# Retention and soft mixture of experts: tiles of 128 positions of one batch in place of 64 positions of two

## The chip, the cores and the metric

The kernel runs on one core of one Trainium2 chip. The metric is the device time of one execution, in microseconds (us). A core has TensorE (PE, matmuls), VectorE (DVE), ScalarE (ACT), GpSimd (POOL) and SyncE (SP, which issues DMAs here). All of them run their own instruction streams and wait for each other by semaphores.

## The reference

`q`, `k` and `v` have 8 batches, 8 heads, 576 positions and 64 features per head, in fp32. The first half is causal attention without softmax, with a decay per head; the second half mixes all 4608 positions into 32 slots, runs 8 experts on 4 slots each, and mixes back:

```
scores = q @ k^T / 8                      # per batch and head
ret    = scores * gamma[h]**(i - j), 0 where j > i
x      = (ret @ v), heads side by side    # 4608 x 512
logits = x @ phi                          # 4608 x 32
d      = softmax of logits over the 4608 positions
slots  = d^T @ x                          # 32 x 512
e_out  = relu(slots[e] @ w1[e]) @ w2[e]   # 8 experts, F = 1024
c      = softmax of logits over the 32 slots
out    = c @ e_out                        # 4608 x 512
```

## The kernel before

**Tiles.** There are 36 tiles of 128 rows. A tile is 64 positions of two batches: rows 0 to 63 belong to one batch, 64 to 127 to the other. The order (`tile_order`) alternates between two pairs of batches. Each tile has 768 KB: keys (`kn`), queries transposed by the host (`qT`), values (`vn`). Four buffers `qb` take them in turn.

**One tile in the loop** (`for i in range(NT)`, L291):
- `k_transpose(i + 1)` (L138): four 128x128 transposes on PE into a `pt` buffer (pool `ps_t`, two buffers), and an ACT copy to `kts`.
- `scale` (L130): POOL multiplies the values by a decay table in place (L133), and builds a second table `xts` (L135) for every other tile.
- `inter` (L145): state of all earlier chunks times queries, 16 small matmuls in two calls, on quadrants of PE (64 rows by 64 columns); it is left out in the first chunk of a batch.
- `scores` (L159): 16 matmuls on quadrants, and a DVE multiplication by the causal mask (L168) to `sts`.
- `values` (L172): 16 matmuls on quadrants with the masked scores, on top of `inter`'s result; DVE multiplies by `xts` on the way out (L183) into a ring of eight tiles.
- `state` (L188): 16 matmuls on quadrants, keys times values, added up in PSUM; ACT copies the state to `sbs` (L203).

In fp32 each matmul call is two PE matmul instructions with a weight load each, and a transpose is one.

**One group of four tiles.** The soft mixture follows four tiles behind. In tile r of the next group:
- r = 0: `logits` (L220, four column strips), then the running maximum and `expo` on DVE and ACT (L238, with `alpha` in L241 and the running sum in L242)
- r = 1: `e_transpose` (L245)
- r = 2: `comb_1` (a transpose of the logits, then DVE and ACT up to the exponential) and at the tile's end `comb_2` (four DVE operations, L276 to L280)
- r = 3: `comb_3` first (the transpose L284 of the result `cn`, and an ACT copy), and at the tile's end `slot_sums` (L254, four column strips)

One `x_transpose` (L209, ACT copy L213) runs in each tile.

**What sets the order.** The schedule is manual: each engine runs its instructions in the order in which the program lists them. SP issues the load of tile i + 4 at the end of tile i, once `state` has read the buffer, and weight units (512 KB each) at a pace of 28 in 32 tiles. 39 of the 64 units are loaded before the expert stage; each unit used there makes room for another.

**Behind the loop** come the last group (logits, transposes, slot sums, the final softmax), the first expert layer (L419), the second (L440), and 18 `final` steps (L451), each with four calls on PE, an ACT copy, a DVE copy and an output DMA.

Of the kernel before, what the change touches and what calls it, by code (L numbers as in the profile page):

```python
# [20 lines left out]
NCH = S // 64  # L21
# [3 lines left out]
NW = 35  # L25
NR = 8
PACE = 30
# [3 lines left out]
def tile_order():  # L31
    return [(p0 + j, c) for p0 in (0, 2) for c in range(NCH) for j in range(2)]


@with_exitstack
def retention_softmoe(ctx, tc, qkv, wts, phi, mtab, vtab, gtab, ctab, msel, out):
# [10 lines left out]
    ps_t = ctx.enter_context(tc.tile_pool(name="ps_t", bufs=2, space=PS))  # L47
# [4 lines left out]
    qb = [const(f"qb{i}", 1536) for i in range(NQ)]  # L52
# [3 lines left out]
    kts = [const(f"kt{i}", 512) for i in range(2)]  # L56
    sts = [const(f"st{i}", 512) for i in range(2)]
    sbs = [const(f"sb{i}", 512) for i in range(2)]
    xts = [const(f"xt{i}", NP, 64) for i in range(2)]
    mt = const("mt", 64)  # L60
    vt = const("vt", NCH, H)
    gt = const("gt", NP, 64)
# [7 lines left out]
    ens = const("ens", P)  # L70
    nrun = [const(f"nrun{i}", 1) for i in range(2)]
    lrun = const("lrun", 1)

    nw = [0]

    def load_w(t):
        if nw[0] < 64:
            nc.sync.dma_start(out=t, in_=wts[nw[0]])
            unit_tile.append(t)
            nw[0] += 1  # L80
            return True
# [13 lines left out]
    load_t(2)  # L95
    load_t(3)
    load_w(ws[1])
# [6 lines left out]
    for _ in range(8):  # L104
        nc.tensor.matmul(pw[:, 0:P], lhsT=wz, rhs=wz, start=True, stop=True)

    def kn(t):
        return qb[t % NQ][:, 0:512]

    def qT(t):  # L110
        return qb[t % NQ][:, 512:1024].rearrange("p (a z i) -> p a z i", a=NP, z=2)

    def vn(t):
        return qb[t % NQ][:, 1024:1536].rearrange("p (h d) -> p h d", h=H)

    R = [slice(0, D), slice(D, P)]
    kT, sT, SX, xT = {}, {}, {}, {}
    sb = {}

    def S_of(t):  # L120
        return SX[t][:, :, 0:256].rearrange("p b (a i) -> p b a i", a=NP)

    def X_of(t):
        return SX[t][:, :, 256:512].rearrange("p b (s i) -> p b s i", s=NP)

    def alloc(t):
        if t not in SX:
            SX[t] = ps_x.tile([P, 2, 512], F32, name="sx")

    def scale(t):  # L130
        c = order[t][1]
        v = vn(t)
        nc.gpsimd.tensor_tensor(out=v, in0=v, in1=vt[:, c, :].unsqueeze(2).broadcast_to([P, H, D]), op=ALU.mult)  # L133
        if t % 2 == 0:
            nc.gpsimd.tensor_tensor(out=xts[t // 2 % 2], in0=gt, in1=cf[:, c, :].unsqueeze(2).broadcast_to([P, NP, 64]),  # L135
                                    op=ALU.mult)

    def k_transpose(t):  # L138
        pt = ps_t.tile([P, 512], F32, name="pt")
        for a in range(NP):  # L140
            nc.tensor.transpose(pt[:, a * P:(a + 1) * P], kn(t)[:, a * P:(a + 1) * P], ident)  # L141
        nc.scalar.copy(out=kts[t % 2], in_=pt)  # L142
        kT[t] = kts[t % 2].rearrange("p (a z s) -> p a z s", a=NP, z=2)

    def inter(t, swap):  # L145
        p, c = order[t]
        if c == 0:
            return
        alloc(t)
        x = X_of(t)  # L150
        sv = sb[p % 2].rearrange("p (z a d) -> p z a d", z=2, a=NP)
        for a0 in (0, 2):
            for j in range(2):
                z = j ^ swap
                for a in (a0, a0 + 1):
                    nc.tensor.matmul(x[R[a % 2], z, 2 * j + a // 2, :], lhsT=sv[R[j], z, a, :], rhs=qT(t)[R[j], a, z, :],  # L156
                                     start=(swap == 1 and a0 == 0), stop=True, skip_group_check=True)

    def scores(t):  # L159
        alloc(t)  # L160
        sp = S_of(t)
        for a in range(NP):
            for j in range(2):
                for z in range(2):
                    nc.tensor.matmul(sp[R[z], 1 - j, a, :], lhsT=kT[t][R[j], a, z, :], rhs=qT(t)[R[j], a, z, :],  # L165
                                     start=(order[t][1] == 0 and a == 0), stop=True, skip_group_check=True)
        st = sts[t % 2].rearrange("p (b a i) -> p b a i", b=2, a=NP)
        nc.vector.tensor_tensor(out=st, in0=sp, in1=mt.unsqueeze(1).unsqueeze(1).broadcast_to([P, 2, NP, 64]),  # L168
                                op=ALU.mult)
        sT[t] = st  # L170

    def values(t):  # L172
        c = order[t][1]
        x = X_of(t)
        v = vn(t)
        for j in range(2):
            for a0 in (0, 2):
                for z in range(2):
                    for a in (a0, a0 + 1):
                        nc.tensor.matmul(x[R[a % 2], z, 2 * j + a // 2, :], lhsT=v[R[z], 2 * a + j, :],  # L180
                                         rhs=sT[t][R[z], 1 - j, a, :], start=False, stop=True, skip_group_check=True)
        xT[t] = ring[t % NR]
        nc.vector.tensor_tensor(out=xT[t].rearrange("p (s z i) -> p z s i", s=NP, z=2), in0=x,  # L183
                                in1=xts[t // 2 % 2].unsqueeze(1).broadcast_to([P, 2, NP, 64]), op=ALU.mult)

    pst = {}

    def state(t):  # L188
        p, c = order[t]
        if c == NCH - 1:  # L190
            return
        if c == 0 and p % 2 == 0:
            pst[0] = ps_st.tile([P, 2, 2, NP, D], F32, name="pst")
        s = pst[0][:, :, p % 2]
        k = kn(t).rearrange("p (h d) -> p h d", h=H)
        v = vn(t)
        for a in range(NP):
            for z in range(2):
                for j in range(2):
                    nc.tensor.matmul(s[R[j], z, a, :], lhsT=k[R[z], 2 * a + j, :], rhs=v[R[z], 2 * a + j, :],  # L200
                                     start=(c == 0 and p % 2 == 0 and a == 0), stop=True, skip_group_check=True)
        sb[p % 2] = sbs[p % 2]
        nc.scalar.copy(out=sbs[p % 2].rearrange("p (z n) -> p z n", z=2), in_=s.rearrange("p z a d -> p z (a d)"))  # L203
# [83 lines left out]
    cn = const("cn", P)  # L287
    k_transpose(0)
    scale(0)
    scores(0)  # L290
    for i in range(NT):  # L291
        g, r = divmod(i - 4, 4)
        if g >= 0:
            if r == 0:
                logits(g)
            elif r == 1:
                e_transpose(g)
            elif r == 2:
                comb_1(g)
            else:  # L300
                comb_3(g)
# [3 lines left out]
        if g >= 0:  # L305
            x_transpose(i - 4)
            if r == 0:
                expo(g)
        inter(i, 0)
        values(i)  # L310
        if i + 1 < NT:
            inter(i + 1, 1)
        state(i)
        if i + 1 < NT:
            scores(i + 1)
        if g >= 0:
            if r == 2:
                comb_2(g)
            if r == 3:
                slot_sums(g)  # L320
# [222 lines left out]
```

## Time and profile before

| | |
|---|---|
| runs shown | 285.41 us median of 3, 283.62 to 285.42 |
| the profiled execution | 285.16 us |
| its span, first to last instruction | 283.4 us |
| PE busy | 216.8 us, 77% of the span |
| DVE, ACT, POOL busy | 93.1, 87.2, 51.5 us |
| mean granted PE clock | 0.869 of full speed |
| moved by DMA | 72.47 MB, 256 GB/s on average |

A line of the profile names the kernel's line, the engine, the operation, and the tiles written and read. PE is the matmul and PEld its weight load, which overlap. A busy PE is not PE at its peak, since matmuls are pipelined and their ends are modelled. "Issue" is time in which an engine waited for nothing that the profile shows. The clock has two levels, 1.2 and 2.4 GHz; a granted clock between them is a mean over time.

### The profile page before, as it was taken

To read this page: it belongs to the slowest core of one execution; us is meant where nothing else is said; L and a number is where in the kernel's file an instruction comes from. 1 tells how busy PE (TensorE), PEld (TensorE's weight loads), DVE (VectorE), ACT (ScalarE), POOL (GpSimd) and SP (SyncE) were. 2 spreads that over 40 slices of the span, in tenths; PEclk is the share of its full clock that TensorE was granted. 3 is DMA by queue.
4 is the path that set the end of the run, shared out by engine and by line. 5 is a ranking of instruction groups with operands and counts; after the bars stand their busy time and mean duration, and the time that the engine had idled before them with its cause. 6 is when DMAs were issued, how large, how long until landed. Compare 5 with 4: busy or idle time off the path is not lost.

```text
span 283.4 us, 12138 instructions
## 1 busy us (share of the span) xinstructions
PE 216.8 (77%) x5594; PEld 157.7 (56%) x5594; DVE 93.1 (33%) x193; ACT 87.2 (31%) x192; POOL 51.5 (18%) x63
## 2 busy tenths in 40 slices
PE   6776977787857976856697588784694989898793
PEld 6665766665647765745676466664562224443451
DVE  0232233335423354522253343341455001033331
ACT  2131533343422243422253334242141000134321
POOL 1533223121321233221112132130021000000000
PEclk9597797999985697997799999899797799999655
DMA  6977685467774478555566749789220499999985
GB/s 212 415 286 242 209 335 193 182 221 273 275 279 158 161 229 324 189 187 187 187 205 234 248 180 289 269 301 388 97 79 1 140 415 407 408 409 412 422 358 225
DMA packets 18196, 72.47 MB, mean 256 GB/s; under 512 B 2401, under 2 KB 2785, under 8 KB 18145
## 3 DMA queue, kind: packets, MB, share of 16 engines
q1 hardware_dynamic: 17568, 71.47, 68.9%
q8 instruction: 44, 0.72, 1.0%
q10 hardware_dynamic: 576, 0.22, 0.3%
q14 instruction: 8, 0.06, 0.1%
HBM read 62.25 MB, written 9.44 MB: 253 GB/s over the span
## 4 chain that ended last, share of the span: by engine, by line
PE 70%; issue 12%; DVE 11%; ACT 3%; DMA 2%; SPq 0%; ACTq 0%; DVEq 0%
PE sx L156 8%; PE sx L180 7%; PE sx L458 7%; PE sx L165 7%; PE pt L209 7%; PE pst L200 7%; PE pst L419 6%; PE pt L141 5%; PE pt L440 5%; DVE st L168 5%; PE pt L254 4%; PE pt L224 3%; DMA qb<-in_qkv 2%; PE pt L284 1%; DVE csm L277 1%
## 5 line engine op out<-in xcount | busy, mean ns | idle before, releaser
L133 POOL TENSOR_TENSOR qb<-qb,vt 128x512 f32<-128x512 f32 x36 | 37.5, 1042 | 134.4 <-DMA qb<-in_qkv 110.9
L183 DVE TENSOR_TENSOR rg<-sx,xt 128x512 f32<-128x512 f32 x36 | 24.8, 690 | 65.8 <-PE sx L180 65.8
L168 DVE TENSOR_TENSOR st<-sx,mt 128x512 f32<-128x512 f32 x36 | 24.9, 691 | 48.9 <-PE sx L165 48.9
L165 PE MATMUL sx<-qb,kt 64*64 64x64 f32 x1152 | 29.0, 237 | 11.6 <-issue 10.9
L203 ACT COPY sb<-pst 128x512 f32<-128x512 f32 x32 | 18.7, 585 | 53.8 <-PE pst L200 53.8
L200 PE MATMUL pst<-qb 64*64 64x64 f32 x1024 | 26.0, 236 | 12.1 <-issue 12.1
L156 PE MATMUL sx<-qb,sb 64*64 64x64 f32 x1024 | 31.9, 239 | 3.8 <-issue 2.8
L165 PEld LDWEIGHTS sx<-qb,kt 64*64 64x64 f32 x1152 | 25.2, 152 | 12.4 <-issue 11.5
L156 PEld LDWEIGHTS sx<-qb,sb 64*64 64x64 f32 x1024 | 24.0, 147 | 10.9 <-issue 9.1
L141 PE MATMUL pt<-ident,qb 128*128 128x128 f32 x144 | 26.6, 313 | 4.5 <-DMA qb<-in_qkv 2.6
L200 PEld LDWEIGHTS pst<-qb 64*64 64x64 f32 x1024 | 22.2, 151 | 13.1 <-issue 13.1
L180 PE MATMUL sx<-st,qb 64*64 64x64 f32 x1152 | 27.2, 238 | 0.2 <-issue 0.2
L209 PE MATMUL pt<-ident,rg 128*128 128x128 f32 x132 | 23.9, 310 | 4.6 <-DVE cn L270 4.4
L142 ACT COPY kt<-pt 128x512 f32<-128x512 f32 x36 | 20.9, 581 | 18.2 <-PE pt L141 18.2
L180 PEld LDWEIGHTS sx<-st,qb 64*64 64x64 f32 x1152 | 23.8, 154 | 1.5 <-issue 0.8
L458 PE MATMUL sx<-kt,lt 32*128 32x256 f32 x144 | 22.0, 548 | 2.5 <-ACT kt L449 0.9
L141 PEld LDWEIGHTS pt<-ident,qb 128*128 128x128 f32 x144 | 18.9, 159 | 7.5 <-issue 5.2
L209 PEld LDWEIGHTS pt<-ident,rg 128*128 128x128 f32 x132 | 17.0, 159 | 8.5 <-PE pt L141 6.7
L213 ACT COPY rg<-pt 128x512 f32<-128x512 f32 x33 | 19.4, 587 | 2.7 <-PE pt L209 2.5
L458 PEld LDWEIGHTS sx<-kt,lt 32*128 32x128 f32 x144 | 10.9, 233 | 13.4 <-ACT ws L460 6.1
L284 PE MATMUL pt<-ident,cn 128*128 128x128 f32 x9 | 3.3, 365 | 18.6 <-DVE cn L280 18.6
L461 DVE COPY ws<-sx 128x512 f32<-128x512 f32 x14 | 9.7, 692 | 23.1 <-PE sx L458 21.2
(79 smaller groups left out, 188.3 us busy)
## 6 DMA issues: line engine op xcount, KB each, us to landing
ws<-in_wts SPq DMA_DIRECT2D x60, 512.0 KB, 7.0
qb<-in_qkv SPq DMA_DIRECT2D x35, 768.0 KB, 4.7
out<-ws SPq DMA_DIRECT2D x14, 512.0 KB, 9.4
qb<-in_wts SPq DMA_DIRECT2D x4, 512.0 KB, 4.2
out<-qb SPq DMA_DIRECT2D x4, 512.0 KB, 5.2
qb<-in_qkv SPq DMA_DIRECT2D x3, 256.0 KB, 3.3
gt<-in_gtab ACTq DMA_DIRECT2D x1, 128.0 KB, 7.1
ms<-in_msel SPq DMA_DIRECT2D x1, 96.0 KB, 6.3
```

The source lines that it names most:

```text
L133: nc.gpsimd.tensor_tensor(out=v, in0=v, in1=vt[:, c, :].unsqueeze(2).broadcast_to([P, H, D]), op=ALU.mult)
L141: nc.tensor.transpose(pt[:, a * P:(a + 1) * P], kn(t)[:, a * P:(a + 1) * P], ident)
L142: nc.scalar.copy(out=kts[t % 2], in_=pt)
L156: nc.tensor.matmul(x[R[a % 2], z, 2 * j + a // 2, :], lhsT=sv[R[j], z, a, :], rhs=qT(t)[R[j], a, z, :], start=(swap == 1 and a0 == 0), sto ...
L165: nc.tensor.matmul(sp[R[z], 1 - j, a, :], lhsT=kT[t][R[j], a, z, :], rhs=qT(t)[R[j], a, z, :], start=(order[t][1] == 0 and a == 0), stop=T ...
L168: nc.vector.tensor_tensor(out=st, in0=sp, in1=mt.unsqueeze(1).unsqueeze(1).broadcast_to([P, 2, NP, 64]), op=ALU.mult)
L180: nc.tensor.matmul(x[R[a % 2], z, 2 * j + a // 2, :], lhsT=v[R[z], 2 * a + j, :], rhs=sT[t][R[z], 1 - j, a, :], start=False, stop=True, sk ...
L183: nc.vector.tensor_tensor(out=xT[t].rearrange("p (s z i) -> p z s i", s=NP, z=2), in0=x, in1=xts[t // 2 % 2].unsqueeze(1).broadcast_to([P, ...
L200: nc.tensor.matmul(s[R[j], z, a, :], lhsT=k[R[z], 2 * a + j, :], rhs=v[R[z], 2 * a + j, :], start=(c == 0 and p % 2 == 0 and a == 0), stop ...
L209: nc.tensor.transpose(pt[:, a * P:(a + 1) * P], xT[t][:, a * P:(a + 1) * P], ident)
L213: nc.scalar.copy(out=xT[t], in_=pt)
L458: nc.tensor.matmul(po[i // 2][:, i % 2, 0:W], lhsT=lt[r, g, :], rhs=so[r, lo:hi], start=True, stop=True, tile_position=(i * NS, 0), skip_g ...
```

## The change

A tile is now 128 positions of one batch. Chunks 0 to 3 of a batch have such tiles, alternately for the two batches of a pair (z = 0, 1); chunk 4 has the last 64 positions of both batches (z = 2). There are still 36 tiles.

- Scores: the 128x128 matrix of a head lies in quadrants. Where the keys are the tile's later half, only the later half of the queries is computed (64 columns instead of 128). The host swaps the key halves of every second pair of heads, so that these blocks take turns between the column halves of PE. The block left out is set to zero once, by DVE. The mask is two DVE operations of 128x512.
- `values` and `state` use all 128 rows: 8 calls each, with 64 output partitions, 128 and 64 columns.
- `inter` is 8 calls of 128 columns (16 of 64 in chunk 4), in one call, in front of `values`.
- Buffers: scores and results each have a fixed pair of PSUM banks; `kts` and `sts` are single; `pt` has three buffers; the state has one bank. `qb` is one large buffer with four slots.
- Order in a tile: `scores(i)`, `inter(i)`, `k_transpose(i + 1)`, group work, `values(i)`, `state(i)`. `comb_3` of a group runs at the next group's r = 0. The x-transposes of a group run two by two at r = 1 and r = 2, `slot_sums` at r = 3 ahead of `values`.
- One weight unit per tile; 45 units are loaded before the expert stage (38 buffers, six parts of `qb`, `sts`).
- The mask table grows from 32 to 256 KB, the decay table `gt` from 128 to 256 KB.

```diff
-NCH = S // 64
+NCH = 5
-NW = 35
+NW = 38
-PACE = 30
 def tile_order():
-    return [(p0 + j, c) for p0 in (0, 2) for c in range(NCH) for j in range(2)]
+    for p in range(B // 2):
+        order += [(p, c, z) for c in range(NCH - 1) for z in range(2)] + [(p, NCH - 1, 2)]
...
-    ps_t = ctx.enter_context(tc.tile_pool(name="ps_t", bufs=2, space=PS))
+    ps_t = ctx.enter_context(tc.tile_pool(name="ps_t", bufs=3, space=PS))
-    qb = [const(f"qb{i}", 1536) for i in range(NQ)]
+    qb = const("qb", NQ * 1536)
-    kts = [const(f"kt{i}", 512) for i in range(2)]
-    sts = [const(f"st{i}", 512) for i in range(2)]
+    kts = const("kts", 512)
+    sts = const("sts", 1024)
...
     load_t(1)
     load_w(ws[0])
     load_t(2)
+    load_w(ws[1])
     load_t(3)
-    load_w(ws[1])
+    load_w(ws[2])
+    load_w(ws[3])
...
+    sp = ps_x.tile([P, 2, NP, P], F32, name="sx")
+    xp = ps_x.tile([P, 2, 2, 2, P], F32, name="sx")
+    pst = ps_st.tile([P, 2, NP, D], F32, name="pst")
+    for a in range(NP):
+        r = slice(0, D) if a % 2 else slice(D, P)
+        nc.vector.memset(sp[r, :, a, 0:D], 0.0)
...
     def scores(t):
         for a in range(NP):
             for j in range(2):
                 for z in range(2):
-                    nc.tensor.matmul(sp[R[z], 1 - j, a, :], lhsT=kT[t][R[j], a, z, :], rhs=qT(t)[R[j], a, z, :], ...)
+                    far = z != a % 2
+                    lo = D if far else 0
+                    nc.tensor.matmul(sp[R[z], j, a, lo:P], lhsT=kT[R[j], a, z * D:(z + 1) * D], rhs=qT(t)[R[j], a, lo:P], ...)
-        nc.vector.tensor_tensor(out=st, in0=sp, in1=mt..., op=ALU.mult)
+        for j in range(2):
+            nc.vector.tensor_tensor(out=sT[:, j]..., in0=sp[:, j]..., in1=m, op=ALU.mult)
+    def X_of(t):
+        return xp[:, :, t % 2]
+    def inter(t):
+        for y in ((z,) if z < 2 else (0, 1)):
+            cols = slice(0, P) if z < 2 else R[y]
+            for a in range(NP):
+                for j in range(2):
+                    nc.tensor.matmul(x[R[a % 2], j, a // 2, cols], lhsT=sb[R[j], y, a, :], rhs=qT(t)[R[j], a, cols], ...)
     def values(t):
         for j in range(2):
+            for a in range(NP):
+                nc.tensor.matmul(x[R[a % 2], j, a // 2, :], lhsT=vn(t)[:, 2 * a + j, :], rhs=sT[:, j, a, :], ...)
     def state(t):
         for a in range(NP):
+            for j in range(2):
+                nc.tensor.matmul(pst[R[j], z, a, :], lhsT=kn(t)[:, 2 * a + j, :], rhs=vn(t)[:, 2 * a + j, :], ...)
+        nc.scalar.copy(out=sb[:, z], in_=pst[:, z])
...
     for i in range(NT):
         g, r = divmod(i - 4, 4)
+        scores(i)
+        inter(i)
         if i + 1 < NT:
             k_transpose(i + 1)
             scale(i + 1)
         if g >= 0:
             if r == 0:
+                if g:
+                    comb_3(g - 1)
                 logits(g)
             elif r == 1:
+                x_transpose(4 * g)
+                x_transpose(4 * g + 1)
                 e_transpose(g)
             elif r == 2:
+                x_transpose(4 * g + 2)
+                x_transpose(4 * g + 3)
                 comb_1(g)
             else:
-                comb_3(g)
+                slot_sums(g)
-        inter(i, 0)
         values(i)
-        if i + 1 < NT:
-            inter(i + 1, 1)
         state(i)
-        if i + 1 < NT:
-            scores(i + 1)
+        if g >= 0:
+            if r == 0:
+                expo(g)
             if r == 2:
                 comb_2(g)
-            if r == 3:
-                slot_sums(g)
         if i + NQ < NT:
             load_t(i + NQ)
-        while nw[0] < min(NW, 2 + (PACE - 2) * (i + 1) // (NT - NQ)):
-            load_w(ws[nw[0]])
+        if len(unit_tile) < NW:
+            load_w(ws[len(unit_tile)])
-    for t in range(NT - NQ, NT):
-        load_w(qb[t % NQ][:, 0:1024])
+    for u in range(6):
+        load_w(qb[:, u * 1024:(u + 1) * 1024])
+    load_w(sts)
...
-    ph = ps_st.tile([P, 2, 512], F32, name="pst")
+    ph = ps_x.tile([P, 2, 512], F32, name="sx")
-    so = cpool.tile([P, 512], F32, name="kt0")
-    p2s = cpool.tile([P, 512], F32, name="kt1")
+    so = kts
+    p2s = xts[0].rearrange("p a i -> p (a i)")
```

## Rows read from the trace of the kernel before

**Rows 1.** The page: the span, and the busy time of PE (us, share of the span, instructions).

```profile
span 283.4 us, 12138 instructions
PE 216.8 (77%) x5594; PEld 157.7 (56%) x5594; DVE 93.1 (33%) x193; ACT 87.2 (31%) x192; POOL 51.5 (18%) x63
```

**Rows 2.** Busy time by stage: the loop, its longest stretch at the low clock, and all that lies behind the loop. Columns: from and to, length, busy us (and instructions) of each engine, then the mean granted clock, the busy share of the DMA engines and GB/s.

```profile
9.05:207.20 198.15, 148.80 (x4928) 124.95 (x4932) 71.24 (x147) 69.14 (x154) 46.96 (x53) 0.88 0.67 237
83.90:98.30 14.40, 12.49 (x309) 10.62 (x309) 4.34 (x9) 3.93 (x8) 2.69 (x3) 0.56 0.43 153
207.20:283.40 76.20, 63.26 (x620) 28.38 (x618) 21.02 (x44) 16.16 (x36) 2.79 (x3) 0.83 0.77 304
```

**Rows 3.** The list of waits, PE alone: who waited for whom, us in total, how often, the longest.

```profile
PE pt L284 <- DVE cn L280: 18.6, 9, 2.8
PE pst L200 <- issue: 12.1, 8, 2.6
PE sx L165 <- issue: 10.9, 5, 3.0
PE pt L209 <- DVE cn L270: 4.4, 7, 0.9
PE sx L156 <- issue: 2.8, 4, 1.3
...
PE pt L141 <- issue: 1.8, 2, 1.3
```

**Rows 4.** The timeline of PE, where a stall ended at 82.2 and from 117 us: start, length, what ran, how many instructions in a row, and in brackets the idle time before it and what ended it. L209 and L141 are transposes, L156 `inter`, L180 `values`, L200 `state`, L165 `scores`.

```profile
82.21 0.34 PE L165 MATMUL sx<-qb,kt 64*64 64x64 f32 x7 [2.44 <-issue]
...
117.37 0.60 PE L209 MATMUL pt<-ident,rg 128*128 128x128 f32 x4
117.90 0.46 PE L156 MATMUL sx<-qb,sb 64*64 64x64 f32 x16
118.18 0.65 PE L180 MATMUL sx<-st,qb 64*64 64x64 f32 x32
118.65 0.41 PE L156 MATMUL sx<-qb,sb 64*64 64x64 f32 x16
118.88 0.65 PE L200 MATMUL pst<-qb 64*64 64x64 f32 x32
119.35 0.29 PE L165 MATMUL sx<-qb,kt 64*64 64x64 f32 x6
121.69 0.68 PE L165 MATMUL sx<-qb,kt 64*64 64x64 f32 x26 [2.05 <-issue]
122.29 0.33 PE L247 MATMUL pt<-ident,ets 128*128 128x128 f32 x1
122.45 0.60 PE L141 MATMUL pt<-ident,qb 128*128 128x128 f32 x4
122.97 0.66 PE L209 MATMUL pt<-ident,rg 128*128 128x128 f32 x4
...
124.54 0.63 PE L200 MATMUL pst<-qb 64*64 64x64 f32 x28
127.25 0.37 PE L200 MATMUL pst<-qb 64*64 64x64 f32 x2 [2.08 <-issue]
```

**Rows 5.** Busy time from the end of one issue stall of PE to the end of the next (columns as in the second group).

```profile
16.02:20.03 4.01, 2.90 (x129) 2.46 (x129) 1.38 (x2) 1.17 (x2) 1.61 (x2) 1.00 0.69 235
20.03:25.66 5.63, 2.89 (x128) 2.49 (x128) 1.38 (x2) 1.17 (x2) 1.04 (x1) 0.93 0.91 318
121.68:127.25 5.57, 3.49 (x127) 2.96 (x127) 1.38 (x2) 1.43 (x3) 1.65 (x2) 1.00 0.51 205
127.25:134.90 7.65, 4.96 (x127) 4.14 (x127) 1.87 (x4) 1.95 (x4) 1.04 (x1) 0.78 0.49 173
```

**Rows 6.** The timeline of PE where slot sums (L254) and logits (L224) follow each other; both use four column strips of 32.

```profile
114.91 1.07 PE L254 MATMUL pt<-rg,ens 128*32 128x512 f32 x8
115.80 1.06 PE L224 MATMUL pt<-rg,phs 128*32 128x128 f32 x32
```

**Rows 7.** The timeline of all engines, from a tile's mask to the transpose of the combine weights.

```profile
108.10 0.69 DVE L168 TENSOR_TENSOR st<-sx,mt 128x512 f32<-128x512 f32 x1 [0.17 <-PE sx L165]
...
110.23 0.29 DVE L280 TENSOR_TENSOR cn<-cn,cri 128x128 f32<-128x128 f32 x1
...
110.67 0.45 PE L284 MATMUL pt<-ident,cn 128*128 128x128 f32 x1 [2.65 <-DVE cn L280]
```

**Rows 8.** Groups of instructions by line: count, busy us, mean ns of one, idle time before them and what ended it.

```profile
L133 POOL TENSOR_TENSOR qb<-qb,vt 128x512 f32<-128x512 f32 x36 | 37.5, 1042 | 134.4 <-DMA qb<-in_qkv 110.9 <-PE pt L141 8.8 <-PE sx L180 8.4
L168 DVE TENSOR_TENSOR st<-sx,mt 128x512 f32<-128x512 f32 x36 | 24.9, 691 | 48.9 <-PE sx L165 48.9
L135 POOL TENSOR_TENSOR xt<-gt,cf 128x256 f32<-128x256 f32 x18 | 11.0, 612 | 6.7 <-DVE rg L183 5.0 <-DMA gt<-in_gtab 1.7
```

**Rows 9.** The timeline at the start: the first tile's key transposes, its value scaling, and the second tile's key transposes.

```profile
4.51 0.60 PE L141 MATMUL pt<-ident,qb 128*128 128x128 f32 x4
...
6.65 1.04 POOL L133 TENSOR_TENSOR qb<-qb,vt 128x512 f32<-128x512 f32 x1 [5.35 <-DMA qb<-in_qkv]
...
9.05 1.09 PE L141 MATMUL pt<-ident,qb 128*128 128x128 f32 x4 [2.57 <-DMA qb<-in_qkv]
```

**Rows 10.** What waited for the weight units that L78 loads: us in total, times.

```profile
  DVE ws L461: 1.9, 2
```

More of the change, by code (lines that the diff above doesn't have):

```diff
@@ L126, in alloc, with xtab @@
[L126 to L128 removed]
+    kT = kts.rearrange("p (a i) -> p a i", a=NP)
+    sT = sts.rearrange("p (j a i) -> p j a i", j=2, a=NP)
+    sb = sbs.rearrange("p (z a d) -> p z a d", z=2, a=NP)
+    xT = {}
+    def xtab(t):
+        p, c, z = order[t]
+        return xts[(p * NCH + c) % 2]
     def scale(t):
[L131 removed]
+        p, c, z = order[t]
         v = vn(t)
         nc.gpsimd.tensor_tensor(out=v, in0=v, in1=vt[:, c, :].unsqueeze(2).broadcast_to([P, H, D]), op=ALU.mult)
[L134 to L135 removed]
+        if z == 0:
+            nc.gpsimd.tensor_tensor(out=xtab(t), in0=gt, in1=cf[:, c, :].unsqueeze(2).broadcast_to([P, NP, P]),
@@ L140, in k_transpose @@
         for a in range(NP):
[L141 to L157, printed above, removed]
+            nc.tensor.transpose(pt[:, a * P:(a + 1) * P], part(t, 0)[:, a * P:(a + 1) * P], ident)
+        nc.scalar.copy(out=kts, in_=pt)
     def scores(t):
-        alloc(t)
-        sp = S_of(t)
         for a in range(NP):
@@ new lines, in scores @@
+                    lo = D if far else 0
+                    nc.tensor.matmul(sp[R[z], j, a, lo:P], lhsT=kT[R[j], a, z * D:(z + 1) * D], rhs=qT(t)[R[j], a, lo:P],
+                                     start=True, stop=True, skip_group_check=True)
+        m = mt[:, 1 if order[t][2] == 2 else 0].unsqueeze(1).broadcast_to([P, 2, 2, P])
+        for j in range(2):
+            nc.vector.tensor_tensor(out=sT[:, j].rearrange("p (s o) i -> p s o i", s=2),
+                                    in0=sp[:, j].rearrange("p (s o) i -> p s o i", s=2), in1=m, op=ALU.mult)
@@ new lines, in X_of @@
+    def X_of(t):
+        return xp[:, :, t % 2]
+    def inter(t):
+        p, c, z = order[t]
+        if c == 0:
+            return
+        x = X_of(t)
+        for y in ((z,) if z < 2 else (0, 1)):
+            cols = slice(0, P) if z < 2 else R[y]
+            for a in range(NP):
+                for j in range(2):
+                    nc.tensor.matmul(x[R[a % 2], j, a // 2, cols], lhsT=sb[R[j], y, a, :], rhs=qT(t)[R[j], a, cols],
+                                     start=(a < 2 and y == (0 if z == 2 else z)), stop=True, skip_group_check=True)
@@ L172, in values @@
     def values(t):
-        c = order[t][1]
+        p, c, z = order[t]
         x = X_of(t)
-        v = vn(t)
         for j in range(2):
[L177 to L181, printed above, removed]
+            for a in range(NP):
+                nc.tensor.matmul(x[R[a % 2], j, a // 2, :], lhsT=vn(t)[:, 2 * a + j, :], rhs=sT[:, j, a, :],
+                                 start=(c == 0 and a < 2), stop=True, skip_group_check=True)
@@ L191, in state @@
+        if z == 2:
             return
[L192 to L196, printed above, removed]
-        for a in range(NP):
[L198 to L201, printed above, removed]
@@ L540 @@
     o = np.asarray(r.results[0]["out_0"]).reshape(2, NG, P, 4, W)
-    x = o.transpose(1, 3, 2, 0, 4).reshape(2, NCH, 2, 2, 64, DM)
-    return np.ascontiguousarray(x.transpose(0, 2, 3, 1, 4, 5)).reshape(B * S, DM)
+    x = o.transpose(1, 3, 2, 0, 4).reshape(NT, P, DM)
+    y = np.empty((B, S, DM), np.float32)
+    for t, (p, c, z) in enumerate(order):
+        if z < 2:
+            y[2 * p + z, c * P:(c + 1) * P] = x[t]
+        else:
+            y[2 * p:2 * p + 2, c * P:] = x[t].reshape(2, D, DM)
+    return y.reshape(B * S, DM)
```

116 lines of the change are left out of this document (54 added, 62 removed).

## The prediction

> **What bounds the kernel now.** I read the page first, for the span and the busy shares, then the busy time by stage, then the list of what TensorE (PE) waited for, and last the timeline, for the stalls and for the pace of each form of matmul. The reader is to see three things.
>
> The retention loop sets the time. It runs from the wait for the second tile (9.05) to the end of the last `values` (207.2): 198.15 us of the 283.4. PE is busy in 148.80 of them, and its mean granted clock is 0.88, which at two levels (1.2 and 2.4 GHz) means about 0.24 x 198 = 47.6 us at the low one. No other engine is busy for half of the loop [rows 1, 2].
>
> PE's 49 idle us in the loop have two main causes. "Issue" holds 12.1 + 10.9 + 2.8 + 1.8 = 27.6 us in 19 pieces, which waited for no engine. The transpose of the combine weights (L284) waits 18.6 us for VectorE (DVE), 2.7 of them behind the loop, so 15.9 in it. L209 adds 4.4 for a `pt` buffer that comb_1 still reads [rows 3].
>
> The issue stalls come in the middle of a group: 6 of 32 score matmuls, then 2.05 us of nothing, then the other 26; next time 28 of 32 state matmuls and 2.08 us [rows 4]. From the end of one such stall to the end of the next there are 127 to 129 matmuls, each time, and as many weight loads: 256 instructions [rows 5]. So I read them as PE waiting for its next block of code. The loop has 4928 matmuls, 38.5 blocks [rows 2]: 0.72 us each on average, over half of the crossings free.
>
> **PE's work.** From start to start at the high clock: 32 matmuls of 64 columns on four quadrants 0.47 us; 16 of them in two parts 0.28 and 0.23; four 128x128 transposes 0.52; a single one 0.16 [rows 4]. Eight matmuls of 512 columns on four column strips, all 128 rows, take 0.89 [rows 6]. In instruction-columns that is 32 x 64 = 2048 in 0.47 and 8 x 512 = 4096 in 0.89: the same 4.4 to 4.6 thousand per us where four run side by side, so 2.2 to 2.3 thousand where two do.
>
> Before, by these: 36 x (0.52 keys + 0.47 scores + 0.47 values) + 32 x (0.51 inter + 0.47 state) + 8 groups x (4 x 0.53 x-transposes + 0.9 logits + 0.9 slot sums + 3 x 0.16 = 4.4) = 52.6 + 31.4 + 35.2 = 119 us. Of the 148.8 busy us that leaves 30: about 47.6 x 0.8 / 2 = 19 for the low clock (PE is busy in 12.49 of the 14.40 us of the longest such stretch [rows 2]) and 11 for handing over.
>
> After, per tile:
> - scores: 16 instructions of 128 columns and 16 of 64 on quadrants, 3072 instruction-columns: 0.70 us, or 0.94 if each set of four waits for its widest. I take 0.80.
> - inter: 16 of 128 columns on quadrants (or 32 of 64 in the last tile of a pair), 0.47, in 28 tiles instead of 32.
> - values: 16 instructions of 128 columns over all rows, two column halves: 2048 at 2.2 thousand, 0.94. State: 16 of 64, 0.47, in 32 tiles. No row shows two column halves. The bounds are 0.94 and 0.47 (side by side, as the strips) and double that (one after the other). I take the first: the strips are the nearest row and also use all 128 rows [rows 6].
> - keys 0.52, group work 35.2 in all, unchanged in count: its transposes move to two tiles of each group, slot sums ahead of `values`.
> - one more change of array form per tile, from values and state back to quadrants. Entering transposes from quadrants costs 0.60 - 26 x 0.015 = 0.2, leaving them nothing visible (0.53 against 0.52) [rows 4]. I take 0.1.
>
> The Trainium skill ("TensorEngine Tiling (Array Packing)", Key Properties) says that a change of tiling mode drains the engine. If every change cost the 0.2 that one of the two directions shows here, 4 us would come on top of my sum; if none but that direction did, 3.6 us would go.
>
> Sum: 36 x (0.80 + 0.47 + 0.52 + 0.94 + 0.47 + 0.1 = 3.30) - 8 x 0.47 - 4 x 0.47 + 35.2 = 148.4 us. PE gets 29 us more to do. The change must win it back from idle time.
>
> **What it takes away.** comb_3 comes a whole tile behind comb_2. That DVE chain ends 1.7 us behind the tile's mask [rows 7], a tile is over 4 us long, so L284 no longer waits: 15.9 us gone. The third `pt` buffer ends L209's wait: 4.4 gone. The instructions: 1600 of the 4928 matmuls go (values 36 x 16, state 32 x 16, inter 32 x 32 - 24 x 16 - 4 x 32), 3328 stay, 26 blocks. A block then holds 148.4 / 26 = 5.7 us of PE work, where it held 119 / 38.5 = 3.1. Stalled blocks followed each other after 4.01, 5.63, 5.57 and 7.65 us [rows 5], so most fetches would be ready or nearly so. Bounds: 0, and 0.72 at each of 26 crossings, 19. I take 8, since the loads are packed denser in a shorter loop.
>
> The Trainium skill ("Runtime: NRT & Kernel Launch", Instruction fetch mechanics) calls the cost of crossing a 16 KiB block mostly hidden. The trace disagrees: 19 of some 38 crossings stall. By the rule the 27.6 us would be something else and might stay whole, which would add 19.6 to my sum.
>
> The low clock: its longest stretches follow idle PE (2.44 us up to 82.2 [rows 4], then low until 98 [rows 2]). With the 20 us of waits gone I take 8 us of loss for 19; bounds 3 and 19.
>
> **What it adds beside PE.** The mask is two DVE operations of 0.69 [rows 8], 1.38 with 0.3 for handing over. Behind it in PE's queue stand only values and state. Ahead of it PE has inter 0.47, keys 0.52 and 0.9 to 1.2 of group work, some 2.1: covered. Not covered are the first four tiles without group work (0.75 each, 3.0), eight tiles whose mask queues on DVE behind comb_2 (0.35 each, 2.8), eight behind the running sum that waits for `alpha` (0.4, 3.2), and eight first tiles of a batch without inter (0.2, 1.6): 10.6 in all, estimates from these lengths, bounds 4 and 15. Inter shares banks with the tile before, whose eviction (0.69, of a mask's size) ends about 1.0 us behind `values`; PE has state and scores, 1.3, in between: nothing. POOL's table doubles, 20 x about 1.04 for 18 x 0.61 [rows 8]; POOL runs tiles ahead, so nothing; if it had no lead, 0.4 us per table, 9 us. Single `kts` and `sts` are refilled only behind their readers in program order: nothing.
>
> `qb` is one buffer now. Waits go by ranges: the first key transposes start at 4.51 while the third part of the same tile lands at 6.65 [rows 9]. So loads still pass readers of other slots.
>
> The start: the mask and decay tables grow by 0.35 MB. At the loop's 237 GB/s [rows 2] that is 1.5 us at most; I take 0.6, so 9.05 becomes 9.6 [rows 9]. Memsets of the score banks lie in that wait. On SP's queue one weight unit more stands ahead of the fourth tile's load and two more ahead of the fifth's: 1.6 MB, 6.6 us at that rate. The fifth tile is first read three tiles later, some 12 us, so nothing; without that cover 6 us, once.
>
> Handing over: 8 (was 11; one DVE wait per tile where there were two).
>
> **Behind the loop** nothing moves but one comb_3 transpose. Six more weight units lie in the buffers beforehand, but PE never waited for a unit there; only two DVE copies did, 1.9 us [rows 10]. So 76.2 us as before.
>
> **Sum.** 9.6 + (148.4 - 0.8 for the first scores, done in the wait + 8 fetch + 8 clock + 10.6 masks + 8) = 191.8; + 76.2 = 268.0 of span. The profiled execution took 285.16 for its span of 283.4, so + 1.8: 270 us. It stands within 0.1% of the median (285.41); the runs spread over 0.6%, so about 1% can be told from no change.
>
> **Rivals.**
> A. Fetches cost as much per crossing as now: 19 instead of 8, 281 us. For it: 7.65 us between two stalls with a half idle DMA (share 0.49) [rows 5], which more cover would not have met. Against: most crossings were free.
> A2. The issue stalls do not go by the number of instructions and stay whole, 27.6: 289. Against: their steps of 256 instructions [rows 5].
> B. The clock falls as often as now: 19 instead of 8, 281. For it: once low it stayed low through 14 us with PE nearly always busy [rows 2]. Against: the waits before it go.
> C. All cover holds: fetch 2, clock 3, masks 4, scores at 0.70: 21 less, 249 us.
> D. Slower: the two column halves don't run side by side. Values become 1.88, state 0.94: 36 x 0.94 + 32 x 0.47 = 49 us more, 319. It decides from 0.3 us more per values group (52 such shares make the 15 us gained). For it: no row has this form, and weights of 128 rows might load singly. Against: the strips.
> E. `qb` is tracked whole, and each tile waits for the newest load: 3 us or more per tile, 370. Only [rows 9] speak, and against it.
>
> **How the numbers follow.** Forecast 0.50 (its own range 262 to 278), A 0.15, A2 0.03, B 0.10, C 0.15, D 0.06, E 0.01. The range from 255 to 284 leaves out the better half of C, and A2, D, E. Faster by over 1% (below 282.6): the forecast, C, and two thirds of A and B, 0.82; within 1%: 0.07; slower: A2, D, E and an edge, 0.11.
>
> **What would show it.** Right: no idle ahead of L284; issue stalls under 12 us in all, still 128 matmuls apart; values at 0.9 to 1.0 us per tile; scores 0.7 to 0.9; a mean granted clock in the loop above 0.92; the loop's end near 192 and 76 us behind it. Wrong: values near 1.9 (D); stalls of 1 us at most crossings (A); clock at 0.88 (B); PE waiting for masks in every tile, which would mean that I mis-sized the cover.

## The result, and the profile after

The changed kernel takes 241.68 us, median of four runs (241.03 to 244.65), against 285.42 in the runs beside it: a ratio of 0.846, 95% interval 0.840 to 0.852. The forecast was 270.0 and its range ended at 255 below: right in direction, 28 us short in size. The profiled execution took 241.08 for a span of 239.3. Runs of one kernel differ from each other: beside the experiments below, on three other chips, the kernel before took 276.33 to 290.76 us, so each median there comes with its range, and the changed kernel's 241.68 is from the first chip.

The page, with the slices of the granted clock, the chain that ended last, and the mask's group. They answer to [rows 1] and [rows 8]:

```profile
span 239.3 us, 8975 instructions
PE 218.5 (91%) x3994; PEld 160.2 (67%) x3994; DVE 115.8 (48%) x233; ACT 78.0 (33%) x192; POOL 61.1 (26%) x65
...
PEclk9999999999999999999999999999958999999855
...
PE 86%; DVE 3%; DMA 3%; ACT 3%; issue 2%; SPq 1%; DVEq 0%; ACTq 0%
...
L166 DVE TENSOR_TENSOR sts<-sx,mt 128x512 f32<-128x512 f32 x72 | 46.3, 684 | 18.7 <-PE sx L162 18.6
```

PE is about as busy as before (218.5 for 216.8 us), in 44 us less. So the gain is idle time, and not busy time that PE was spared. The stages say where, in the columns of [rows 2]: the loop, its first 4.85 us, and all that lies behind it.

```profile
9.34:164.40 155.06, 150.81 (x3332) 127.22 (x3332) 93.43 (x183) 59.70 (x153) 57.51 (x57) 1.00 0.87 317
...
9.34:14.19 4.85, 4.85 (x69) 4.33 (x69) 0.69 (x1) 0.96 (x2) 3.72 (x4) 1.00 1.02 422
...
164.40:239.30 74.90, 61.49 (x611) 27.36 (x611) 20.26 (x43) 16.43 (x37) 1.86 (x3) 0.86 0.71 279
```

The loop gave 43.1 of the 44.1 us of span. PE's idle time in it fell from 49.4 to 4.25 us, and the granted clock rose from 0.88 to 1.00, which by the two levels is 48 us at 1.2 GHz before and none that the row shows now (the first 4.85 us are a case of their own, below). PE's list of waits (us in total, times, the longest) has nearly lost the rows of [rows 3]:

```profile
PE pt L284 <- DVE cn L280: 2.4, 1, 2.4
PE sx L181 <- issue: 2.4, 2, 1.4
...
PE sx L189 <- DVE sts L166: 1.2, 2, 0.8
...
PE sx L162 <- issue: 0.7, 2, 0.5
```

The one wait of L284 that is left is the last group's, behind the loop. Issue stalls are 3.1 us in four pieces, where there were 27.8 in 20 (the prediction's 27.6 in 19 leaves out one of 0.2). The masks (L189 waits for `sts`) cost 1.2 us in all.

The timeline of all engines shows PE's pace and why the mask is late so seldom:

```profile
80.26 1.09 PE L189 MATMUL sx<-sts,qb 128*64 128x128 f32 x16
...
81.18 0.63 PE L201 MATMUL pst<-qb 128*64 128x64 f32 x16
...
81.74 0.90 PE L162 MATMUL sx<-qb,kts 64*64 64x128 f32 x32
...
82.46 0.65 PE L181 MATMUL sx<-qb,sbs 64*64 64x64 f32 x32
...
82.84 0.45 DVE L242 SCALAR_TENSOR_TENSOR lrun<-lrun,alpha,rs 128x1 f32<-128x1 f32 x1 [0.75 <-ACT alpha L241]
83.04 0.66 PE L153 MATMUL pt<-ident,qb 128*128 128x128 f32 x4
...
83.21 1.27 DVE L166 TENSOR_TENSOR sts<-sx,mt 128x512 f32<-128x512 f32 x2
...
83.54 1.04 PE L209 MATMUL pt<-ident,rg 128*128 128x128 f32 x8
...
84.41 0.30 PE L247 MATMUL pt<-ident,ets 128*128 128x128 f32 x1
...
84.64 1.09 PE L189 MATMUL sx<-sts,qb 128*64 128x128 f32 x16
```

From start to start, `values` take 0.92 us and scores 0.72. This is a tile in which the mask queues on DVE behind the running sum (L242, which itself waited 0.75 us for `alpha`). It starts at 83.21 and ends at 84.48; `values` start at 84.64 with no wait, because PE had inter, key transposes and group work to do from 82.46 on.

### The profile page after: what moved, and what is told of

Its sections match the earlier page's. It is cut to its first block, busy times and chain, and to the rows that moved or that the text cites. A ratio compares the mean times of both kernels' runs of the same rounds, so it can differ in the third digit from the quotient of the medians.

```text
span 239.3 us, 8975 instructions
## 1 busy us (share of the span) xinstructions
PE 218.5 (91%) x3994; PEld 160.2 (67%) x3994; DVE 115.8 (48%) x233; ACT 78.0 (33%) x192; POOL 61.1 (26%) x65
## 4 chain that ended last, share of the span: by engine, by line
PE 86%; DVE 3%; DMA 3%; ACT 3%; issue 2%; SPq 1%; DVEq 0%; ACTq 0%
PE sx L189 16%; PE sx L162 12%; PE pt L153 8%; PE sx L455 8%; PE sx L416 7%; PE pst L201 6%; PE pt L437 6%; PE pt L209 6%; PE sx L181 6%; PE pt L224 4%; PE pt L254 4%; DMA qb<-in_qkv 3%; ACT ws L457 1%; PE pt L265 1%; PE pt L445 1%
## 5 line engine op out<-in xcount | busy, mean ns | idle before, releaser
L141 POOL TENSOR_TENSOR qb<-qb,vt 128x512 f32<-128x512 f32 x36 | 37.5, 1043 | 86.7 <-DMA qb<-in_qkv 63.0
L166 DVE TENSOR_TENSOR sts<-sx,mt 128x512 f32<-128x512 f32 x72 | 46.3, 684 | 18.7 <-PE sx L162 18.6
L189 PE MATMUL sx<-sts,qb 128*64 128x128 f32 x576 | 40.4, 283 | 1.2 <-DVE sts L166 1.2
L189 PEld LDWEIGHTS sx<-sts,qb 128*64 128x64 f32 x576 | 31.4, 139 | 12.6 <-issue 7.8
L154 ACT COPY kts<-pt 128x512 f32<-128x512 f32 x36 | 21.1, 586 | 56.7 <-PE pt L153 54.9
L162 PE MATMUL sx<-qb,kts 64*64 64x64 f32 (+1 forms) x1152 | 34.0, 255 | 1.4 <-issue 0.7
L162 PEld LDWEIGHTS sx<-qb,kts 64*64 64x64 f32 x1152 | 28.0, 137 | 5.0 <-issue 1.7
L203 ACT COPY sbs<-pst 128x256 f32<-128x256 f32 x32 | 11.9, 372 | 36.7 <-PE pst L201 36.7
L455 PE MATMUL sx<-kts,lt 32*128 32x256 f32 x144 | 19.9, 503 | 3.0 <-ACT ws L457 1.9
L201 PE MATMUL pst<-qb 128*64 128x64 f32 x512 | 20.7, 224 | 0.0
L181 PE MATMUL sx<-qb,sbs 64*64 64x128 f32 (+1 forms) x512 | 18.4, 258 | 2.4 <-issue 2.4
L201 PEld LDWEIGHTS pst<-qb 128*64 128x64 f32 x512 | 19.8, 141 | 0.0
L455 PEld LDWEIGHTS sx<-kts,lt 32*128 32x128 f32 x144 | 9.8, 215 | 12.9 <-ACT ws L457 9.5
L209 PE MATMUL pt<-ident,rg 128*128 128x128 f32 x132 | 17.2, 273 | 0.0
L457 ACT COPY ws<-sx 128x512 f32<-128x512 f32 x18 | 10.5, 586 | 18.7 <-PE sx L455 17.6
```

Of the source, the lines that this page charges most:

```text
L154: nc.scalar.copy(out=kts, in_=pt)
L162: nc.tensor.matmul(sp[R[z], j, a, lo:P], lhsT=kT[R[j], a, z * D:(z + 1) * D], rhs=qT(t)[R[j], a, lo:P], start=True, stop=True, skip_group_ ...
L166: nc.vector.tensor_tensor(out=sT[:, j].rearrange("p (s o) i -> p s o i", s=2), in0=sp[:, j].rearrange("p (s o) i -> p s o i", s=2), in1=m, ...
L181: nc.tensor.matmul(x[R[a % 2], j, a // 2, cols], lhsT=sb[R[j], y, a, :], rhs=qT(t)[R[j], a, cols], start=(a < 2 and y == (0 if z == 2 else ...
L189: nc.tensor.matmul(x[R[a % 2], j, a // 2, :], lhsT=vn(t)[:, 2 * a + j, :], rhs=sT[:, j, a, :], start=(c == 0 and a < 2), stop=True, skip_g ...
L201: nc.tensor.matmul(pst[R[j], z, a, :], lhsT=kn(t)[:, 2 * a + j, :], rhs=vn(t)[:, 2 * a + j, :], start=(c == 0 and z == 0 and a == 0), stop ...
```

## The experiments

The theory (T1): in the kernel before, waits of 1 to 3 us in the loop were paid twice, once themselves and once in the clock that fell behind them. The change removes most of the waits, by combining a tile later and by issuing 1600 matmuls less, each with its weight load, so the clock stays up and PE is the bound. The rival (T2): the later combine step alone, or the new form of the scores alone, makes the gain, and the clock merely goes with PE's share of busy time. The scores can be ruled out at once, since they take longer per tile than before (0.72 us from start to start, where 32 such matmuls took 0.47 before [rows 4]).

**1. The kernel before, with the later combine step alone.** In the old loop over tiles, comb_3 of a group moves to the first tile of the next:

```diff
+                if g:
+                    comb_3(g - 1)
 ...
-            else:
-                comb_3(g)
 ...
+    comb_3(NG - 2)
```

> The kernel before, with comb_3 of a group moved to r = 0 of the next group, ahead of its logits; nothing else. Theory 1 (the low clock and part of the fetch stalls hang on how long PE stands still): the wait ahead of L284 goes (15.9 us in the loop), part of it comes back as issue stalls since blocks of 256 instructions are used up sooner, and the clock in the loop rises from 0.88 to 0.92 or more: 263 to 272 us. Theory 2 (the clock rose because values and state now use all 128 rows): the clock stays at 0.88, and the kernel gains the wait alone less what fetches take back: 272 to 278 us.

It took 275.57 us (269.48 to 277.76; the kernel before on that chip 286.91). The waits, and the loop:

```profile
PE sx L165 <- issue: 12.0, 6, 2.7
PE pst L200 <- issue: 9.0, 8, 2.5
PE sx L180 <- issue: 5.5, 4, 1.8
PE sx L156 <- issue: 4.9, 4, 2.3
...
PE pt L141 <- issue: 3.4, 2, 2.6
...
PE pt L224 <- ACT lt L285: 2.9, 8, 0.4
```

```profile
9.48:199.50 190.02, 146.56 (x4932) 118.84 (x4932) 71.00 (x149) 68.57 (x153) 47.02 (x54) 0.92 0.71 247
```

All 15.9 us of waits for the combine weights left the loop, but the issue stalls grew from 27.8 in 20 pieces to 34.8 in 24, and the logits now wait 2.9 us for the copy of the combine weights that stands ahead of them. The loop won 8.1 us, and the lowest times differ by as much (269.48 and 277.65). So part of what a removed wait gives comes back as waiting for code; that a block could arrive while PE stood for DVE would explain it, and is not shown. The time lies in the range of the second theory expected above (272 to 278), and the clock of 0.92 is the least that the first had asked for: the time at the low level fell by some 17 us in the loop, PE's busy time by 2.2 only. That a wait is paid twice does not show here. The combine step alone is a fifth to a quarter of the gain.

**2. The changed kernel, with the combine step put back** ahead of the scores of the group's last tile:

```diff
+        if g >= 0 and r == 3:
+            comb_3(g)
 ...
-                if g:
-                    comb_3(g - 1)
 ...
-    comb_3(NG - 2)
```

> The kernel after, with comb_3 back at the start of the tile behind comb_2 (r = 3), ahead of the scores. The DVE chain ends about 1.3 us behind the start of those scores, so 8 waits of 1.2 to 1.6 us come back, 11 us. Theory 1: the clock falls with them in places, 3 to 8 us more, 255 to 261 us, clock in the loop 0.93 to 0.97. Theory 2: the clock stays at 1.00 and the cost is the waits alone, 249 to 253 us.

256.51 us (256.07 to 258.27), 15 more than the changed kernel.

```profile
PE pt L284 <- DVE cn L280: 16.9, 9, 2.6
...
PE sx L181 <- issue: 1.7, 1, 1.7
```

```profile
9.41:181.60 172.19, 154.90 (x3338) 128.70 (x3338) 95.04 (x183) 60.70 (x154) 57.65 (x57) 0.98 0.81 287
```

The loop is 17.1 us longer. Eight waits in it hold 14.5 us, and a clock of 0.98 means about 7 us at the low level, where T1 had expected 0.93 to 0.97: waits of this size cost the clock less here than in the kernel before. Of the 17.1 us, 13.0 are idle and 4.1 busy time. Issue stalls did not come back with the waits (2.4 us in two pieces).

**3. The same tile, another place.** comb_3 stays in the group's last tile, but stands behind the score and inter work, just ahead of the slot sums:

```diff
-                if g:
-                    comb_3(g - 1)
 ...
+                comb_3(g)
                 slot_sums(g)
 ...
-    comb_3(NG - 2)
```

> The kernel after, with comb_3 in the tile behind comb_2 (r = 3), but behind scores, inter and the key transposes, just ahead of slot_sums. The chain that ends in cn ends about when the key transposes do, so L284 should wait 0.2 us or less: 241 to 244 us by both theories. If the move to the next group itself was what counted, this one would lose 10 us or more.

244.03 us (239.80 to 244.33), the changed kernel's time within the spread.

```profile
PE pt L284 <- DVE cn L280: 3.7, 2, 2.4
```

In the loop L284 waits once, 1.3 us; the other 2.4 are the last group's. What counts is the PE work that stands between the DVE chain and the transpose, not that the step moves into the next group.

**4. The changed kernel with its instructions back.** Each matmul of 128 columns in scores, inter and values becomes two of 64; the combine step stays late:

```diff
-  nc.tensor.matmul(sp[R[z], j, a, lo:P], ..., rhs=qT(t)[R[j], a, lo:P], ...)
+  for lo in ((D,) if far else (0, D)):
+      nc.tensor.matmul(sp[R[z], j, a, lo:lo + D], ..., rhs=qT(t)[R[j], a, lo:lo + D], ...)
 ...
```

> The kernel after, with every matmul of 128 columns in scores, inter and values issued as two of 64: the same columns in the same array forms, but some 1540 PE matmuls and as many weight loads more, nearly the number of before. Theory 1, code fetch: a block of 256 instructions then holds some 3.9 us of PE work instead of 5.8, issue stalls return at 0.4 to 0.8 us per crossing, 15 to 28 us, and with them some low clock: 258 to 280 us. Rival (the stalls hung on the order of the work or on the loads' timing, not on the number of instructions): up to 5 us for the extra weight loads, 242 to 247 us.

281.23 us (277.50 to 285.00; before 286.91). Two stretches from stall to stall, and the loop:

```profile
75.04:80.49 5.45, 4.53 (x129) 3.95 (x128) 2.84 (x6) 1.96 (x7) 1.87 (x2) 1.00 0.62 224
80.49:86.60 6.11, 4.33 (x127) 4.02 (x127) 2.21 (x4) 1.73 (x4) 1.25 (x2) 1.00 0.54 209
...
9.26:200.00 190.74, 168.07 (x4852) 145.08 (x4852) 94.50 (x183) 60.47 (x153) 57.88 (x57) 0.97 0.73 259
```

```profile
PE sx L162 <- issue: 5.9, 5, 1.7
PE sx L181 <- issue: 5.3, 6, 1.7
PE pst L203 <- issue: 4.2, 2, 2.4
```

The issue stalls are back, 21.9 us in 19 pieces, again 127 to 129 matmuls, or a multiple of that, apart. The same columns in more instructions cost the loop 35.7 us: 18.8 of stalls, some 5 by the clock (11 us at the low level, at 0.8 busy and half speed), and the rest, some 12, because two matmuls of 64 columns take longer than one of 128 (about 0.3 us per tile). This is the largest part of the gain, and the rival's 242 to 247 falls. Theory 1's range, which ended at 280, had no term for these 12.

**5. The other way round in `values`:** each pair of heads reads the second half of the mask first.

```diff
-        for j in range(2):
-            for a in range(NP):
+        for a, j in [(a0 + o, j) for a0 in (0, 2) for j in (1, 0) for o in range(2)]:
+            if True:
```

> The kernel after, with the matmuls of values in an order that reads the second mask operation's half first, so that PE waits for both (2 x 0.69 us) where it waits for the first alone in the kernel after. Theory M (the masks cost PE 1.2 us and not the predicted 10.6 because half of the mask work lies beside the first half of values): waits of L189 for DVE return, 0.3 to 0.7 us in the first four tiles and in the tiles behind comb_2 and the running sum, 5 to 10 us in all, 246 to 252 us. Rival (the group work covers both operations anyway): 241 to 243 us, waits under 3 us.

242.71 us (240.89 to 246.11). L189 now waits 3.9 us for the mask, in seven places, for 1.2 in two:

```profile
PE sx L189 <- DVE sts L166: 3.9, 7, 1.3
```

So reading the early half first hides 2.7 us, not the 9 that would have explained my mask term. The rest was never there: PE's work covers both halves. Three of the seven waits are in the first tiles, which have no group work (0.61, 0.47 and 0.29 us, where the prediction had 0.75 each); the other four lie in later tiles.

**6. Both put back:** 2 and 4 together, with the diffs of those.

> The kernel after with both earlier edits: comb_3 ahead of the scores behind comb_2, and all 128-column matmuls issued as two of 64. PE should stand still about 14 us for L284 and 15 to 22 us for code, some 32 to 36 us of the loop, between the kernel before (49) and the split one (22), but in the array forms of the kernel after. Theory 1 (the time at the low clock goes with the time PE stands still, in any form): 18 to 32 us at the low clock in the loop (mean granted clock 0.92 to 0.96). Theory 2 (the new forms keep the clock up): under 12 us, 0.97 or more. Time: 290 to 302 us.

294.30 us (284.76 to 296.29; before 283.28 on that chip). The loop:

```profile
9.63:218.50 208.87, 173.78 (x4852) 148.60 (x4852) 96.99 (x183) 61.38 (x154) 57.54 (x56) 0.94 0.67 237
```

35.1 us of idle, and 25 us at the low clock, where the two single edits had 7 and 11: more than their sum in this execution. The mean clock over its span is 0.916, and in the four runs 0.916 to 0.948, so the 25 are not a fixed price. In time the two edits cost together what they cost singly (53 us, for 15 and 40). The tiles of 128 with neither gain are no faster than the kernel before.

Of T1 this shows the first half: the place of the combine step and the count of instructions make the gain, and T2's combine step alone does not. The second payment, in the clock, is small where rows show it: 4.1 us of busy time in experiment 2, some 5 (an estimate) in 4, 2.2 in 1.

**7. The kernel before without weight loads in the loop.** They are put off behind it:

```diff
-        while nw[0] < min(NW, 2 + (PACE - 2) * (i + 1) // (NT - NQ)):
-            load_w(ws[nw[0]])
```

> The kernel before, with no weight unit loaded inside the loop beyond the two at its start; the other units are loaded at the loop's end, so the whole kernel gets longer behind the loop and only the loop counts here. If a block of code comes late because its fetch stands behind the tile loads in the DMA queues, the issue stalls (27.6 us in 19 pieces) fall to 5 to 15 us with 40% fewer bytes per tile, and the loop from 198 to 175 to 188 us. If the fetch has a fixed latency of its own, they stay at 22 to 30 us.

One run, 280.43 us, with a loop of 184.85. Up to 175, ahead of the first stall behind the start of the put-off loads (168.4), the loop and its waits (the list is of the whole span):

```profile
9.05:175.00 165.95, 132.21 (x4623) 110.43 (x4624) 65.59 (x136) 64.66 (x145) 46.83 (x53) 0.95 0.51 176
```

```profile
PE sx L165 <- issue: 11.6, 7, 4.7
PE pst L200 <- issue: 6.2, 6, 2.1
PE sx L156 <- issue: 2.6, 4, 1.0
```

Up to the 36th block the stalls are 14.6 us in 15 pieces (with one of 0.5 ahead of L180), for 22.5 in 18 before. The next one, with the put-off loads under way, is 4.7 us. So code seems to wait partly behind data, but more than half of the stalls stay without it. In the whole loop they are 20.9 us, between the two ranges that were expected (5 to 15, and 22 to 30). It isn't load that the change took away: its loop moves 317 GB/s and has 3.1 us of stalls.

**8. Six preloaded units.** The changed kernel with 39 weight units instead of 45 before the loop's end; the last six are loaded behind it:

```diff
-NW = 38
+NW = 35
 ...
-    for u in range(6):
+    for u in range(4):
 ...
-    load_w(sts)
```

> The kernel after, with 39 weight units loaded ahead of the expert stage, as before, in place of 45 (35 buffers, four parts of qb). The prediction took the six units as worth nothing: 241 to 243 us, the stretch behind the loop 74 to 77 us. Rival (they relieve the saturated DMA in the expert stage): that stretch grows by 3 to 8 us, 245 to 250 us.

241.07 us (240.34 to 243.01). The part behind the loop is 74.80 for 74.90: those units are worth nothing, as the prediction had it.

```profile
163.70:238.50 74.80, 61.28 (x613) 27.55 (x611) 20.27 (x43) 16.44 (x37) 1.95 (x3) 0.87 0.76 303
```

**9. Two `pt` buffers instead of three:**

```diff
-    ps_t = ctx.enter_context(tc.tile_pool(name="ps_t", bufs=3, space=PS))
+    ps_t = ctx.enter_context(tc.tile_pool(name="ps_t", bufs=2, space=PS))
```

> The kernel after, with two pt buffers instead of three. The prediction put the third buffer at 4.4 us (the wait of L209 before). In the order of the kernel after, the tiles r = 1 and r = 2 fill three or four pt buffers within 1.7 us while ACT needs 0.59 us to empty one: the second x-transpose and the fourth filling should wait 0.3 to 0.5 us each. Theory 1 (idle time brings the low clock): 16 tiles x 0.6 to 0.9 us, 10 to 14 us, and little low clock since each wait is short: 250 to 257 us. Rival (ACT's copies keep up): 246 us or less.

253.48 us (253.43 to 254.51). 12 us, where the wait that the third buffer was to end held 4.4 before [rows 3]. In the new order the transposes follow each other more closely, and several lines wait:

```profile
PE pt L224 <- ACT kts L154: 4.7, 7, 0.9
PE pt L209 <- ACT kts L154: 4.3, 16, 0.3
...
PE sx L189 <- DVE sts L166: 1.8, 3, 1.0
PE sx L181 <- issue: 1.4, 1, 1.4
```

```profile
9.40:176.40 167.00, 154.13 (x3333) 126.14 (x3332) 94.56 (x184) 61.28 (x153) 57.42 (x57) 1.00 0.82 293
```

12.9 us of idle, in pieces of at most 1.4 us, and the row's clock stays at 1.00. The loop is 11.9 us longer, 8.6 of them idle; that PE is busy 3.3 us longer is not explained.

**10. A version that beats both.** With the loop full, the end shows: in the last output steps of the changed kernel PE waits for copies (L455 for L457, 1.9 us in four pieces). Every other one of them gets banks of its own, which the loop has left free:

```diff
+        if k == 1 and g % 2 == 1:
+            pb = [ps_st.tile([P, 512], F32, name="pst")] + [ps_t.tile([P, 512], F32, name="pt") for _ in range(3)]
+            ...
```

> The kernel after, with every second output step of the last nine in a second set of PSUM banks (the state's bank and the three of pt), so that its matmuls do not wait for the copies of the step before. These steps take 1.4 to 1.9 us each in the kernel after, PE and copies one behind the other, with PE at the low clock for most of them (0.50 to 0.59). With two sets a step should take the longer of matmuls (0.64 to 1.25) and copies (0.7 to 0.85): 3 to 7 us less, 235 to 239 us. Rival (the output DMAs, 512 KB each, bound this stretch): 240 to 242 us.

236.32 us (234.64 to 238.21), about 5 us less than the change as it was made. The stretch from 218 to the end, first in the changed kernel, then in this one:

```profile
218.00:239.30 21.30, 14.04 (x74) 7.17 (x74) 6.31 (x10) 6.00 (x11) 0.00 (x0) 0.67 0.64 261
```

```profile
218.00:234.50 16.50, 7.04 (x74) 5.01 (x74) 6.11 (x13) 5.51 (x14) 0.00 (x0) 0.80 0.81 324
```

The same 74 matmuls keep PE busy for half the time, at a higher mean clock (0.80 for 0.67). So more went than the 1.9 us of waits; how much of it is the clock is not shown.

## Why the prediction was wrong in size

The span was put at 268.0 and is 239.3. Term by term, with the difference that each made:

- **PE's work, right.** 148.4 us were predicted, 147.6 of them in the loop. Measured: 155.06 of loop less 4.25 idle and some 2 us of slow first tiles (below) leave 148.8. The bet inside it held: `values` take 0.92 to 0.94 us from start to start (0.94 predicted), so the two column halves run side by side and rival D falls. Scores take 0.72 (0.83 into key transposes), state 0.56 into scores. E falls too: PE waits for loads of `qb` once, 1.4 us at the start.
- **Masks, 10.6 predicted, 1.2 measured: 9.4 us.** I added up the tiles whose cover was short by 0.2 to 0.75 us, as if each part of PE's work ended just when its group's cost said. Experiment 5 shows that PE could even read the wrong half first and lose only 2.7 us more. It was the step "Not covered are ..." that failed, and the bound of 4 below was too high as well.
- **Handing over, 8 predicted, at most 1.2 measured (148.8 less 147.6): 6.8 us.** The prices were taken from start to start, which holds the handing over already; then I added 0.1 per tile for the form's change and 8 us more. That is a term counted twice. The 11 us from which it came were a remainder in the kernel before, and no run here says of what. Where experiment 4 brings the narrow matmuls back, a similar remainder returns, which points at them and is no more than that.
- **Clock, 8 predicted, 2 measured: 6 us.** The granted clock of the loop is 1.00, but the first tiles cost 2 us: the first `values` took 1.77 us, and most other forms up to 14.19 about double. In experiment 10 the same first `values` took as long (10.40 to 12.16) where the row shows 0.50, and in experiment 3, at 1.00, they took 0.92 (10.04 to 10.96). So I count the 2 us as the low clock, though the row of the changed kernel does not show it.
- **Code fetch, 8 predicted, 3.1 measured: 4.9 us.** 26 blocks of 5.7 us of work each came in time but for four. The reason given for 8, loads packed denser in a shorter loop, failed: they are denser (317 for 237 GB/s), and the stalls went all the same. Rival A (0.72 us per crossing as before) had the number of crossings right and their price wrong; the "most crossings were free" against it was half of them, by the prediction's own count. Experiment 4 shows that A2 was wrong as well, since stalls go with the count of instructions. The Trainium skill ("Runtime: NRT & Kernel Launch", Instruction fetch mechanics) has a crossing mostly hidden: that agrees with the changed kernel and disagrees with experiment 4, where the same columns in 38 blocks stall for 21.9 us.
- **Start and end, right:** 9.34 for 9.6, and 74.90 for 76.2, together 1.6 us.

These make 9.4 + 6.8 + 6 + 4.9 + 1.6 = 28.7, the difference of the spans. The mechanism was the predicted one, and the sign-posts for it came out (no idle ahead of L284 in the loop, stalls under 12 us, `values` at 0.9 to 1.0, clock above 0.92, 75 us behind the loop); the loop's end was put at 192 and is 164.4. So the path and the work were right, and the side costs were sized too high: handing over was counted twice, and the masks, the clock and the code fetch were each set near the middle of their bounds and came out near or below the lower ones (4, 3 and 0). The runs do not show one condition behind all of them. In experiment 2 the long waits are back and the clock falls in places, but issue stalls are 2.4 us and mask waits 0.3; in experiment 1 a wait that was removed brought more stalls, not fewer. Rival C, in which all cover holds, was this case with a chance of 0.15; it gave 249 since it kept the doubled 8 us.

## What to carry to other kernels

Prices read from start to start already hold the handing over; nothing is added to them. When an engine's own work is known from such prices, give the sum with every side cost at its lower bound beside the sum with each in the middle (here about 249 and 270), and ask of each cost which row holds it up. They need not go together: here mask waits went with the work ahead of their reader (experiment 5), stalls with the count of instructions (experiment 4), and the low clock with idle time. And where stalls come at equal counts of instructions, the same columns in fewer, wider instructions can be worth more than the column count says: 35.7 us of loop here.

## What the runs showed that was not expected

**The low clock goes with the idle time of the loop, but not wait by wait.** Idle time in the loop against the time at the low level, 2 x (1 - clock) x length: experiment 9: 12.9 us, none; experiment 2: 17.3, 7 us; experiment 4: 22.7, 11; experiment 6: 35.1, 25; experiment 1: 43.5, 30; the kernel before: 49.4, 48. Both forms of the loop lie on about one rising line, so nothing here points at the form of the matmuls as what holds the clock up. Each point is one execution, and the first two leave out some 5 us at the start that ran at half pace, as in the changed kernel. The length of a wait does not decide alone either. In experiment 2 the clock stayed up behind the longest wait for the combine weights and fell behind a shorter one (a wait and its stretch, twice):

```profile
79.90 0.30 PE L284 MATMUL pt<-ident,cn 128*128 128x128 f32 x1 [2.55 <-DVE cn L280]
77.00:84.00 7.00, 4.45 (x93) 3.04 (x91) 4.69 (x8) 1.23 (x3) 2.52 (x3) 1.00 0.71 249
...
98.76 0.30 PE L284 MATMUL pt<-ident,cn 128*128 128x128 f32 x1 [2.00 <-DVE cn L280]
98.00:105.00 7.00, 6.24 (x103) 4.29 (x107) 3.28 (x7) 1.23 (x3) 2.21 (x4) 0.76 0.56 205
```

What decides between the two is open.

**A removed wait came back, mostly as code.** Of 15.9 us of waits taken from the kernel before, 7.0 returned as issue stalls and 2.9 as waits of the logits (experiment 1).

**A buffer's worth depends on the order around it:** 4.4 us of waits before, 12 us after (experiment 9).
